# Attention and gated convolution on one core: batch 1's convolution on VectorE, in another written order of all engines

## The chip, the cores and the metric

The kernel runs on one core of a Trainium2 chip. The metric is the device time of one execution in microseconds (us), as the median of several runs. The core's engines are TensorE (PE in the profile, with its weight loads as PEld), VectorE (DVE), ScalarE (ACT), GpSimd (POOL) and SyncE (SP). Each works through its own queue in order; POOL and SP issue the transfers.

## The reference

There are 8 batches of 8 heads, 576 positions and 64 features a head; the feed-forward part has 1024 hidden features and a convolution of three taps. All inputs and the output are float32.

```python
def _attn_ref(q, k, v, g_norm):
    kv = np.einsum('bhsd,bhse->bhde', k, v)
    out = np.einsum('bhsd,bhde->bhse', q, kv)
    rms = np.sqrt(np.mean(out * out, axis=-1, keepdims=True) + 1e-06)
    return (out / rms * g_norm).astype(np.float32)

def _moe_ref(x, w_in, conv_w, w_out):          # x: (8, 576, 512), the heads side by side
    h = np.maximum(x @ w_in, 0.0)              # (8, 576, 1024)
    hp = ...                                   # h with one row of zeros ahead and behind
    for k in range(3):
        conv_out += conv_w[k][None, None, :] * hp[:, k:k + S, :]
    gate = 1.0 / (1.0 + np.exp(-conv_out))
    return (h * gate @ w_out).astype(np.float32)
```

## The kernel before

The whole program is one string of step names, `ORDER`, read from left to right. Each name calls a small function which issues its instructions, and at the end every engine is bound to the order in which it was given them. A name is a step with its indices; `@` gives the buffers or PSUM banks it takes, and `:` chooses an engine. So `kv.3.0.4@2` is the key-value product of batch 3, head pairs 0 to 3, into bank 2. A bank (there are eight) is free again when the step that empties it has run.

The steps, in the order in which one batch meets them (b is the batch, t a pair of heads, f a block of 128 hidden features, p a pair of batches):

- `Lq`, `Lk`, `Lv` load q, k and v of a batch (POOL issues them and they are cast to bfloat16 on the way, L301); `Li`, `Lo` load quarters of w_in and halves of w_out (L315, L322). Two buffers each for q, k and v are reused by later batches, so such a load waits for the last step that reads the buffer.
- `qt` (L380) transposes q on PE and `qc` copies the result out of PSUM; `qtp` (L388) is another form for batch 4. For batches 5 to 7 `dq` does it instead by a transposing transfer that SP issues (L436), behind the load of q.
- `kv` (L358) is k times v, 48 matmuls for a batch; `kvc`, `kvn`, `ky` copy it out, `kx` moves halves of it by a transfer.
- `ot` (L430, L431) or `oq` (L464) is q times that. `sq` (L493) squares it on ACT and `oc` copies it to SBUF.
- The norm: for batches 0 and 1 `on`, `nl`, `mu0`; later `ss` (sums of squares, L575), `ln` (root, L584), `sl` (its split into two bfloat16 parts, four DVE instructions, L591 to L594), `sp` (spreading on PE, L603), `mu` (L629). Batch 7's factors go through DRAM (`fw`, `fr`).
- `hm` (L640) is the hidden product, eight matmuls for a block of a batch; `re` is its relu (L646 on ACT, L648 on DVE).
- The convolution of a block pair on DVE: `ta` (two tap multiplies for a block, L699, L700), `aa` and `ab` (two additions, L706, L712); `sg` is the sigmoid on ACT (L745), `mg` the merge h times gate on DVE (L751). It is done by a group of batches: group 0 is batch 0, group 1 batch 1, group 2 batches 2 and 3, and so on. For blocks 6 and 7 of groups 0 and 1 `cm` (L731) does the convolution on PE with diagonal weights, six matmuls for a block, and `sg` reads PSUM (L742); `dg` makes those weights.
- `om` (L761) is the output product of 128 rows, in two halves of four matmuls for the first and last pair of batches and eight matmuls at once otherwise; `oh` (L776) is the very last one in two halves of its columns. `ea`, `eh` empty it into a row buffer, `st`, `sh` store it by SP.
- `unread` issues matmuls on constant data whose result nobody reads (fills, L427).

The lines by which a step's engine is chosen are these; in `copy` the engine is the caller's choice, which differs from step to step:

```python
    def copy(to, fr, on_act):
        if on_act:
            nc.scalar.activation(to, fr, AX.Copy)
        else:
            nc.vector.tensor_copy(to, fr)
    def relu(to, fr):
        if pick[0] == 0:
            nc.scalar.activation(to, fr, AX.Relu)
        else:
            nc.vector.tensor_scalar(to, fr, 0.0, None, op0=AL.max)
```

For `qc` and `qc0` the choice 1 is ACT; for `kvc`, `kvn`, `ky`, `oc`, `ea` and `eh` it is DVE. Whether a group's block uses the convolution on PE is decided by nothing but whether `cm` stands in the order for it.

Of the kernel before, what the change touches and what calls it, by code (L numbers as in the profile page):

```python
# [72 lines left out]
sqh.0.3.0@3 unread.3@3 onh.0.3.0@6 sqh.0.3.1 onh.0.3.1 nlh.0.3.0@3 muh.0.3.0 Lk.1.0@1 qt.1.0@0 nlh.0.3.1 qc.1.0:1@2
muh.0.3.1 Li.0 hm.0.2@6 re.0.2 ta.0.2@0 hm.0.3@4 re.0.3 hm.0.6@6 Lq.1.2 ta.0.3 Lv.1.2 re.0.6 aa.0.1 hm.0.7@4 Lk.1.2
Lq.2.0@0 cm.0.6@6 re.0.7:1 sg.0.6@1 kv.1.0.2@0 cm.0.7@4 kvc.1.0.2.0:1@1 kvc.1.0.2.1 sg.0.7 ot.1.0@0 hm.0.1@6 ab.0.1
sq.1.0@4 re.0.1 qt.1.1@4 hm.0.0@2 on.1.0@6 mg.0.3 qc.1.1@3 ot.1.1@4 nl.1.0@4 re.0.0:1 sq.1.1@5 kv.1.2.2@2
kvc.1.2.2.0 ta.0.0@1 mu0.1.0 kvc.1.2.2.1 on.1.1@6 Li.2 ot.1.2@2 nl.1.1@5 ot.1.3@0 ta.0.1 sq.1.2@6 mu0.1.1 aa.0.0
# [768 lines left out]
```

## Time and profile before

| what | value |
|---|---|
| median of 3 runs | 179.97 us (179.6 to 180.15) |
| span of the profiled execution | 177.6 us |
| that execution's own time | not recorded apart; the median is 2.4 us above the span |
| PE busy | 168.4 us, 95% of the span |
| ACT busy | 149.7 us, 84% |
| DVE busy | 139.5 us, 79% |
| POOL busy | 30.8 us, 17% |
| granted PE clock | 1.000 |

The span runs from the first to the last instruction of one execution under the profiler. Busy times are unions of instructions of an engine. A row of the chain of waits reads: start, length, what it was (an engine's line, or a transfer). A row of a timeline reads: start, length, engine, line, operation, output and input with their shapes, how many, and in brackets the idle time before it with what ended it. A row of the busy time by stretch reads: the stretch, its length, then the busy time of PE, PEld, DVE, ACT and POOL, the granted clock, the share of the transfer engines and GB/s. A row of the transfers ends with the median time from issue to landing. A row of the waits reads: who waited for whom, in total, how often, the longest.

### The profile page before, as it was taken

Reading aid. Unit: us, or ns where it says so; the run is one execution under the profiler, and the core shown is the slowest. Engines: PE = TensorE matmul, PEld = TensorE weight load, DVE = VectorE, ACT = ScalarE, POOL = GpSimd, SP = SyncE. Lnnn points to the kernel's source line nnn. Section 1 sums busy time; section 2 is a strip of 40 time slices with the busy share of each in tenths; the row PEclk is TensorE's granted clock in tenths of the full one; section 3 lists DMA queues with packets and bytes.
Section 4 is the critical chain, followed back from the end, with each engine's and each line's share of the span. In section 5 each row is a group of like instructions: output and inputs, shape, how many; then the busy total and the mean of one; then the engine's idle time right before and its main releaser. Section 6 shows DMA issues by size and latency. Waiting matters only on the chain.

```text
span 177.6 us, 4060 instructions
## 1 busy us (share of the span) xinstructions
PE 168.4 (95%) x1641; PEld 101.3 (57%) x1660; DVE 139.5 (79%) x235; ACT 149.7 (84%) x233; POOL 30.8 (17%) x54
## 2 busy tenths in 40 slices
PE   6989996999999999999999999999999999999992
PEld 2545753877545677753667764444677764444541
DVE  5665669999998898999799999939999999950000
ACT  2479899999999969999999999999989987764332
POOL 7995516402600013050000000000000000000000
PEclk9999999999999999999999999999999999999999
DMA  6999999999999999999999950197040003422696
GB/s 155 188 183 197 200 204 201 205 203 206 205 204 203 198 192 139 174 203 198 160 201 179 293 128 0 53 219 263 21 160 0 4 0 143 152 82 99 258 352 219
DMA packets 36219, 29.49 MB, mean 166 GB/s; under 512 B 8528, under 2 KB 31720, under 8 KB 36200
## 3 DMA queue, kind: packets, MB, share of 16 engines
q0 software_dynamic: 21760, 15.96, 59.5%
q1 hardware_dynamic: 14400, 13.26, 28.9%
q8 instruction: 13, 0.21, 0.4%
q14 instruction: 6, 0.05, 0.1%
q10 hardware_dynamic: 40, 0.01, 0.0%
HBM read 33.70 MB, written 9.58 MB: 244 GB/s over the span
## 4 chain that ended last, share of the span: by engine, by line
PE 70%; DMA 20%; POOL 4%; ACT 2%; issue 2%; POOLq 0%; ACTq 0%
PE bank L761 33%; PE bank L640 27%; DMA v_sb<-in_v_dram 10%; DMA k_sb<-in_k_dram 7%; DMA q_sb<-in_q_dram 4%; PE bank L358 3%; PE bank L464 2%; POOL q_sb L241 1%; PE bank L603 1%; PE bank L575 1%; POOL v_sb L241 1%; POOL k_sb L241 1%; PE bank L776 1%; PE bank L731 1%; PE bank L388 1%
## 5 line engine op out<-in xcount | busy, mean ns | idle before, releaser
L640 PE MATMUL bank<-xT,w_in_sb 128*128 128x288 bf16 x496 | 64.5, 286 | 0.1
L761 PE MATMUL bank<-w_out_sb,h 128*128 128x512 bf16 x268 | 63.0, 379 | 1.1 <-issue 0.6
L640 PEld LDWEIGHTS <-w_in_sb 128*128 128x128 bf16 x496 | 47.6, 98 | 14.1 <-issue 0.5
L761 PEld LDWEIGHTS <-h 128*128 128x128 bf16 x280 | 26.3, 98 | 30.6 <-issue 1.9
L646 ACT ACTIVATE h<-bank 128x576 bf16<-128x576 f32 x61 | 37.9, 657 | 4.2 <-PE bank L640 3.9
L745 ACT ACTIVATE taps<-taps,cwn 128x1152 bf16<-128x1152 bf16 (+1 forms) x36 | 38.2, 1094 | 0.1
L341 ACT ACTIVATE row<-bank 128x512 f32<-128x512 f32 (+1 forms) x37 | 21.3, 598 | 12.3 <-PE bank L761 9.3
L751 DVE TENSOR_TENSOR h<-h,taps 128x2304 bf16<-128x2304 bf16 (+1 forms) x20 | 22.2, 1113 | 2.0 <-ACT taps L745 1.2
L706 DVE TENSOR_TENSOR taps<-taps 128x2304 bf16<-128x2304 bf16 (+1 forms) x18 | 20.9, 1160 | 0.4
L712 DVE TENSOR_TENSOR taps<-taps,h 128x2304 bf16<-128x2304 bf16 (+1 forms) x18 | 20.8, 1153 | 0.3
L699 DVE TENSOR_SCALAR taps<-h,cwn 128x1152 bf16<-128x1152 bf16 (+1 forms) x36 | 16.7, 463 | 2.5 <-ACT h L646 2.4
L493 ACT ACTIVATE sq<-bank 128x576 bf16<-128x576 f32 x28 | 17.9, 676 | 0.0
L700 DVE TENSOR_SCALAR taps<-h,cwn 128x1152 bf16<-128x1152 bf16 (+1 forms) x36 | 17.5, 487 | 0.0
L629 DVE SCALAR_TENSOR_TENSOR xT<-o,cw,bank 128x576 bf16<-128x576 f32 x20 | 15.3, 809 | 2.7 <-PE bank L603 2.5
L341 ACT ACTIVATE o<-bank 128x576 f32<-128x576 f32 x22 | 15.0, 694 | 0.0
L213 ACT ACT_TABLE_LOAD x10 | 12.8, 1283 | 2.5 <-issue 2.4
L301 POOL DMA_DIRECT2D q_sb<-in_q_dram x8 | 6.2, 772 | 31.4 <-PE bank L388 16.6
L427 PE MATMUL bank<-fill 128*128 128x512 bf16 x25 | 9.0, 480 | 1.7 <-DVE fill L228 1.5
L358 PEld LDWEIGHTS <-k_sb 96*64 96x64 bf16 x384 | 7.3, 114 | 4.0 <-issue 2.6
L358 PE MATMUL bank<-v_sb,k_sb 96*64 96x64 bf16 x384 | 8.5, 199 | 1.0 <-DMA k_sb<-in_k_dram 0.7
L301 POOL DMA_DIRECT2D k_sb<-in_k_dram x8 | 6.1, 758 | 14.4 <-PE bank L358 12.5
L562 DVE SCALAR_TENSOR_TENSOR xT<-bank,cw,root 128x576 bf16<-128x576 f32 x7 | 5.6, 815 | 1.8 <-ACT root L542 1.7
(93 smaller groups left out, 135.3 us busy)
## 6 DMA issues: line engine op xcount, KB each, us to landing
out_dram<-row SPq DMA_DIRECT2D x35, 256.0 KB, 2.8
q_sb<-in_q_dram POOLq DMA_DIRECT2D x6, 576.0 KB, 13.7
k_sb<-in_k_dram POOLq DMA_DIRECT2D x6, 576.0 KB, 14.7
v_sb<-in_v_dram POOLq DMA_DIRECT2D x6, 576.0 KB, 16.3
factor<-factor SPq DMA_DIRECT2D x4, 288.0 KB, 4.9
w_in_sb<-in_moe_w_in_dram POOLq DMA_DIRECT2D x4, 256.0 KB, 8.7
w_out_sb<-in_moe_w_out_dram POOLq DMA_DIRECT2D x2, 512.0 KB, 18.0
q_sb<-in_q_dram POOLq DMA_DIRECT2D x4, 144.0 KB, 4.6
```

What stands on the lines that cost most here:

```text
L341: nc.scalar.activation(to, fr, AX.Copy)
L358: nc.tensor.matmul(ps[i][i * D:(i + 1) * D, t - t0, :], k_sb[:, 2 * t + i, r * D:(r + 1) * D], v_sb[:, 2 * t + i, r * D:(r + 1) * D], star ...
L493: nc.scalar.activation(in_order(b, s), product(b, t), AX.Square)
L640: nc.tensor.matmul(ps[:, e, :HS], w_in_sb[:, t, f * P:(f + 1) * P], x[:, t, e * HS:(e + 1) * HS], start=(t == 0), stop=(t == NT - 1))
L646: nc.scalar.activation(to, fr, AX.Relu)
L699: nc.vector.tensor_scalar_mul(tap[:, 0, f % 2, :n, 8:8 + S], h[:, f], cwn[:, 0, f:f + 1])
L700: nc.vector.tensor_scalar_mul(tap[:, 1, f % 2, :n, :S], h[:, f], cwn[:, 2, f:f + 1])
L706: nc.vector.tensor_add(tap[:, 1, :, :n, :S], tap[:, 0, :, :n, 7:7 + S], tap[:, 1, :, :n, 1:1 + S])
L712: nc.vector.tensor_add(y, y, h[:, 2 * j:2 * j + 2])
L745: nc.scalar.activation(y, y, AX.Sigmoid, scale=cwn[:, 1, f:f + 1])
L751: nc.vector.tensor_mul(h, h, T["tap", c, j][:, 1, :, :n, :S])
L761: nc.tensor.matmul(T["om", p, m], h[:, f, m * P:(m + 1) * P], w_out_sb[:, f, :], start=(f == 0), stop=(f == NF - 1))
```

## The change

Nothing but the string `ORDER` changes; every function stays. Batch 1's blocks 6 and 7 get `ta.1.6`, `ta.1.7`, `aa.1.3` and `ab.1.3` in place of `cm.1.6` and `cm.1.7`, so the whole convolution of batch 1 runs on VectorE. All steps stand in another order, banks and buffers are given out anew, and the loads of POOL and the transposing transfers of SP are in another sequence. The engine is another one for these steps: from ACT to DVE go 14 relus (`re.0.1`, `0.5`, `0.6`, `1.0`, `1.2`, `1.4`, `2.3`, `3.0`, `3.6`, `4.1`, `5.4`, `5.5`, `6.6`, `7.1`), `ea.0.5`, `1.1`, `1.6`, `2.1`, `3.0`, `3.4`, `3.5`, `eh.3.8.0`, `oc.2.3`, `4.3`, `7.1`, `7.3`, `qc0.0.1` to `0.3`, `kvc.1.0.2.1` and `kvn.5`; from DVE to ACT go `oc.2.0`, `oc.5.0`, `qc.2.1`, `qc.4.0`, seven `kvc`, `kvn.6`, `kvn.7` and both `ky.5`. There are 26 fills instead of 27.

POOL's loads after the first ten, before: Lq.1.0 Li.1 Li.3 Lv.1.0 Lk.1.0 Li.0 Lq.1.2 Lv.1.2 Lk.1.2 Lq.2.0 Li.2 Lk.2.0 Lv.2.0 Lq.3.0 Lk.3.0 Lv.3.0 Lo.0 Lo.1 Lq.4.0 Lq.5.0 Lk.4.0 Lv.4.0 Lk.5.0 Lv.5.0 Lq.7.0 Lv.7.0 Lk.7.0 Lk.6.0 Lv.6.0 Lq.6.0.

After: Lq.1.0 Li.3 Li.1 Lk.1.0 Lv.1.0 Lq.1.2 Li.0 Lv.1.2 Lk.1.2 Lq.2.0 Lk.2.0 Lv.2.0 Li.2 Lq.3.0 Lk.3.0 Lv.3.0 Lo.0 Lo.1 Lk.4.0 Lq.5.0 Lv.4.0 Lq.4.0 Lv.5.0 Lk.5.0 Lk.6.0 Lk.7.0 Lv.7.0 Lq.7.0 Lv.6.0 Lq.6.0.

The transposing transfers of SP, before: dq.5.0 dq.5.1 dq.7.0 dq.7.1 dq.6.0 dq.6.1; after: dq.5.1 dq.5.0 dq.7.0 dq.6.0 dq.6.1 dq.7.1.

The diff, cut to the start, the stretch from kv.1.2.2 to batch 1's last taps, the stretch around kv.6.0.4, and the end:

```diff
 ORDER = """
-pre@0,0,0 unread.10@0 qt0.0.0@0 ps pn pi ca.k.0 ca.v.0 kv.0.0.1@1 kvc.0.0.1.0:1@0 ct@2 qt0.0.1@3 qc0.0.0:1@0
...
-hm.0.5@0 sg.0.1 Lk.3.0@1 Lv.3.0@1 re.1.7 sg.0.0 pl ta.1.2@0 re.0.4 ta.1.3 re.0.5 hm.1.4@4 kv.2.0.4@2 Lo.0 aa.1.1
...
-oc.2.1 Lk.4.0@0 Lv.4.0@0 kv.3.0.4@2 re.1.0 ss.2@3 oc.2.3 mg.0.2 ln.8@0 aa.1.2 kvc.3.0.4.0:1@1 kvc.3.0.4.1:1 ab.1.2
...
-om.0.2.0@2 Lv.5.0@1 sg.1.5 sg.1.4 qtp.4.0@0 cm.1.6@6 qc.4.0@4 mg.1.2 ea.0.0@2 hm.2.5@4 sl.1@0 hm.2.2@0 sg.1.1
-om.0.2.4 re.2.5 sg.1.6@0 re.2.2 ea.0.2@3 sg.1.0 sp.3.0@6,4 cm.1.7@0 mu.3.0.1 mu.3.0.0 hm.2.4@2 hm.2.7@6 sg.1.7
...
+pre@0,0,0 ca.k.0 Lq.1.0@1 ca.v.0 pi unread.10@6 kv.0.0.1@0 unread.2@6 ct@1 qt0.0.1@2 al.h0@0 al.x0@0 Li.3 qt0.0.0@3
...
+ab.0.0 mu0.1.3 ps ha.1.2@4 qc.2.0@0 hb.1.2 sg.0.0 re.1.2:1 sg.0.1 hb.1.3 re.1.3 kv.2.0.4@0 mg.0.1 qt.2.1@2
+kvc.2.0.4.0@0 kvc.2.0.4.1 qc.2.1:1@1 ta.1.2@0 hm.0.4@4 ta.1.3 aa.1.1 mg.0.0 ot.2.0@0 ab.1.1 sq.2.0@0 hm.0.5@6 re.0.4
+hm.1.1@2 oc.2.0@0 re.0.5:1 ta.0.4@1 re.1.1:1 ot.2.2@4 sg.1.3 ot.2.1@0 sq.2.2@1 hm.1.4@6 oc.2.2@1 sq.2.1@2 hm.1.7@2
+hm.1.0@4 ta.0.5 re.1.4:1 aa.0.2 oc.2.1 sg.1.2 ot.2.3@0 re.1.7 ab.0.2 hm.1.5@6 qt.3.1@2 re.1.0:1 sq.2.3@3 Lk.3.0@1
+oc.2.3:1 Lv.3.0@1 Lo.0 Lo.1 kv.3.0.4@4 ss.2@5 mg.1.1 sg.0.4 sg.0.5 re.1.5 qt.3.0@0 hm.1.6@6 qc.3.1@0 mg.0.2
...
+re.2.4 hm.2.7@2 hm.2.5@6 re.2.7 mg.1.2 re.2.5 ab.1.0 sp.3.0@0,2 mu.3.0.1 sg.1.1 om.0.2.4 sg.1.0 mu.3.0.0 ta.1.6@0
...
+ab.2.3 hm.2.0@2 ea.0.6@5 re.2.0 aa.2.1 sl.2@0 ab.2.1 hm.3.1@0 sp.4.1@4,2 re.3.1 kv.7.0.4@6 mu.4.1.0 Lq.6.0@0 sg.2.3
+kvn.7.0.4 mu.4.1.1 sp.4.0@0,4 sg.2.2 mu.4.0.0 om.0.8.4 kx.7.0.4.0 hm.3.0@2 mu.4.0.1 al.h2@0 sp.5.0@0,4 kv.6.0.4@6
...
+sg.4.5 sg.4.4 aa.4.3 om.3.6.0@1 om.3.5.0@4 st.2.4 st.1.3 ab.4.3 sg.4.6 om.3.2.0@5 sg.4.7 ea.2.1:1@1 mg.4.2 om.2.6.0@7
+mg.4.3 om.3.1.4 om.3.2.4 om.3.3.4 om.3.6.4 om.3.5.4 st.2.8 st.2.7 ea.3.1@2 om.3.0.4 ea.3.2@4 st.2.3 ea.3.3@0
...
```

More of the change, by code (lines that the diff above doesn't have):

```diff
@@ L73 @@
[L73 to L77, printed above, removed]
@@ new lines @@
+sq.0.1@0 kvc.0.2.1.0 mu0.0.0 pl kvc.0.2.1.1 unread.1@2 on.0.1@0 ot.0.2@2 nl.0.1@1 mu0.0.1 qt0.0.3@4 unread.3@5
+kv.0.3.1@5,0 sq.0.2@0 qc0.0.3 kvc.0.3.1.1:1 Lq.1.2 kvc.0.3.1.0 on.0.2@6 nl.0.2@0 ot.0.3@4 sqh.0.3.0@0 unread.2@0
+onh.0.3.0@0 sqh.0.3.1 mu0.0.2 onh.0.3.1 Li.0 Lv.1.2 nlh.0.3.0@1 nlh.0.3.1 muh.0.3.0 muh.0.3.1 qt.1.0@6 qc.1.0:1@0
+hm.0.6@2 hm.0.2@0 re.0.2 al.h1@1 re.0.6:1 pn hm.0.7@4 hm.0.3@2 Lk.1.2 kv.1.0.2@0 ta.0.2@0 re.0.3 dg.6:1 dg.7:1
+cm.0.6@6 kvc.1.0.2.0@0 re.0.7:1 cm.0.7@2 kvc.1.0.2.1:1 sg.0.6@1 Lq.2.0@0 sg.0.7 qt.1.1@0 ta.0.3 qc.1.1@1 ot.1.0@4
@@ new lines @@
+ea.0.1@0 sp.2.1@2,6 mu.2.1.0 ot.3.3@0 mu.2.1.1 ea.0.3@1 om.0.0.0@5 sq.3.3@3 Lq.5.0@0 aa.1.2 oc.3.3 ss.3@4 sp.2.0@2,6
+mu.2.0.0 om.0.0.4 ln.1@0 ab.1.2 om.0.2.0@4 mu.2.0.1 sg.1.5 hm.2.4@0 Lv.4.0@0 ea.0.0@2 Lq.4.0@1 dq.5.1@2 sl.1@0 sg.1.4
+re.2.4 hm.2.7@2 hm.2.5@6 re.2.7 mg.1.2 re.2.5 ab.1.0 sp.3.0@0,2 mu.3.0.1 sg.1.1 om.0.2.4 sg.1.0 mu.3.0.0 ta.1.6@0
+hm.2.2@6 sp.3.1@2,0 kv.4.0.4@5 re.2.2 al.x2@1 ea.0.2@3 Lv.5.0@1 mu.3.1.1 kvn.4.0.4 qtp.4.1@6 ky.4.0.4.1 qtp.4.0@0
+ky.4.0.4.0 mu.3.1.0 hm.3.4@2 qc.4.0:1@0 hm.3.5@4 ta.1.7 re.3.4 qc.4.1@1 re.3.5 mg.1.0 oq.4.2@0 aa.1.3 ta.2.4@1
@@ new lines @@
+dq.5.0@3 sq.4.2@0 st.0.1 oq.4.0@2 ta.2.5 hm.2.6@6 oc.4.2@0 re.2.6 hm.3.6@4 sq.4.0@1 oc.4.0@1 ab.1.3 aa.2.2 hm.3.3@0
+sg.1.6 re.3.6:1 hm.3.7@6 Lk.5.0@1 re.3.3 om.0.5.0@2 ab.2.2 oq.4.3@0 sg.1.7 oq.4.1@4 mg.1.3 re.3.7 kv.5.0.4@3 sq.4.3@2
+oc.4.3:1 sq.4.1@3 oc.4.1 sg.2.4 kvn.5.0.4:1 ky.5.0.4.0 ky.5.0.4.1 hm.3.2@6 hm.2.3@0 om.0.5.4 ta.2.6@0 re.3.2 Lk.6.0@0
+Lk.7.0@1 om.0.7.0@4 oq.5.0@6 st.0.2 ta.2.7 sg.2.5 re.2.3:1 oq.5.2@0 om.0.7.4 ea.0.5:1@4 sq.5.2@4 aa.2.3 om.0.6.0@5
+oq.5.3@2 oc.5.2@2 sq.5.0@5 oq.5.1@0 Lv.7.0@0 oc.5.0@3 sq.5.3@6 mg.2.2 Lq.7.0@1 om.0.6.4 om.0.4.0@6 ss.4@7 sq.5.1@7
@@ new lines @@
+re.5.3 sq.7.1@1 hm.5.0@0 hm.5.5@6 hm.5.2@2 st.0.0 re.5.0 st.0.7 sg.2.6 aa.2.0 ab.2.0 oc.7.1:1 sg.2.1 sg.2.0 re.5.5:1
+hm.4.1@0 hm.4.5@4 re.4.1:1 kx.6.0.4.0 re.5.2 mg.2.3 hm.5.1@6 hm.5.4@0 re.4.5 st.0.8 mg.2.0 dq.6.1@1 kx.6.0.4.1
+oq.6.2@2 oq.6.0@4 re.5.4:1 re.5.1 sq.6.0@2 ta.3.2@0 hm.5.6@6 ta.3.3 om.1.1.0@0 dq.7.1@2 oc.6.0@1 oq.7.2@4 sq.6.2@3
+st.0.3 re.5.6 oc.6.2@2 aa.3.1 st.0.6 sq.7.2@4 oq.6.1@6 ea.1.1:1@0 oq.7.3@2 sq.6.1@5 ab.3.1 ta.3.0@1 om.1.3.0@1 oc.6.1
+oc.7.2@3 sq.7.3@6 ta.3.1 oq.6.3@6 om.1.6.0@0 oc.7.3:1 ea.1.6:1@1 om.1.5.0@4 sq.6.3@7 aa.3.0 hm.4.7@2 ss.6@0 sg.3.3
@@ new lines @@
+oc.6.3 ea.1.3@2 sg.3.2 mg.3.1 ss.7@1 ln.4@0 fw.4 ta.3.4@0 hm.5.7@6 re.5.7 ta.3.5 ln.3@0 ea.1.5@5 om.1.2.0@5 hm.4.6@6
+ab.3.0 ea.1.2@6 om.1.4.0@0 om.1.7.0@1 al.x3@0 st.1.1 aa.3.2 ea.1.4@0 re.4.7 sl.3@0 sp.6.0@2,4 re.4.6 ab.3.2 ea.1.7@7
+om.1.8.0@0 mu.6.0.0 sg.3.1 fr.7.1@0 sg.3.0 mu.6.0.1 sp.6.1@6,2 mu.6.1.0 mu.6.1.1 om.1.0.0@1 hm.6.0@4 sg.3.4 mu.7.1.0
+hm.6.5@2 fr.7.0@1 mg.3.0 hm.6.3@6 ta.3.6@1 mu.7.0.1 al.h3@1 mu.7.0.0 re.6.0 ta.3.7 st.0.4 hm.6.2@4 st.1.4 re.6.5
+re.6.3 hm.6.4@2 ea.1.8@0 st.1.2 re.6.2 re.6.4 st.0.5 mu.7.1.1 hm.6.1@6 st.1.5 aa.3.3 sg.3.5 st.1.6 hm.7.0@4 ab.3.3
@@ new lines @@
+ea.1.0@1 hm.7.5@2 hm.7.1@0 re.7.0 re.7.5 mg.3.2 re.7.1:1 sg.3.7 sg.3.6 hm.7.3@4 hm.7.2@2 re.6.1 re.7.2 mg.3.3 hm.7.6@0
+ta.4.0@0 re.7.3 ta.4.1 hm.7.4@6 st.1.8 hm.6.6@2 hm.7.7@4 re.7.6 re.7.4 om.2.2.0@0 om.2.5.0@1 om.2.3.0@6 aa.4.0
+re.6.6:1 ab.4.0 ta.4.2@1 sg.4.0 ta.4.3 aa.4.1 om.2.0.0@7 ea.2.3@0 om.2.4.0@6 sg.4.1 re.7.7 ea.2.5@3 ab.4.1 mg.4.0
+ta.4.4@0 hm.6.7@2 ta.4.5 om.2.8.0@1 ea.2.0@4 st.1.7 st.1.0 sg.4.2 sg.4.3 om.2.1.0@7 aa.4.2 ea.2.2@1 mg.4.1 st.2.0
+ta.4.6@1 om.2.7.0@0 ea.2.4@4 st.2.2 om.3.3.0@6 re.6.7 om.3.4.0@2 om.3.1.0@3 ea.2.8@5 ea.2.7@6 ta.4.7 om.3.0.0@0 ab.4.2
```

55 lines of the change are left out of this document (12 added, 43 removed).

## The prediction

> **What bounds the kernel now.** I read the page's head first, then the busy time by stretch, then the chain of waits, then the loads one by one, last the timelines of the engines for the price of single steps. Steps carry the names of the written order (kv.3.0.4 is batch 3's key-value product); a step "after" is one of the changed order.
>
> ```profile
> span 177.6 us, 4060 instructions
> PE 168.4 (95%) x1641; PEld 101.3 (57%) x1660; DVE 139.5 (79%) x235; ACT 149.7 (84%) x233; POOL 30.8 (17%) x54
> core 0: us, PE busy (x) PEld busy (x) DVE busy (x) ACT busy (x) POOL busy (x), PEclk, DMA share, GB/s
> 27.04:45.91 18.87, 17.26 (x264) 12.57 (x268) 18.39 (x35) 18.50 (x33) 7.18 (x17) 1.00 1.32 204
> 45.91:158.30 112.39, 111.32 (x1027) 67.17 (x1039) 103.13 (x145) 106.10 (x161) 6.38 (x8) 1.00 0.79 143
> 45.91:174.29 128.38, 127.17 (x1106) 74.98 (x1119) 103.72 (x145) 112.00 (x172) 6.38 (x8) 1.00 0.77 156
> 15.16 11.83 DMA k_sb<-in_k_dram
> 38.04 0.95 PE L358 MATMUL bank<-v_sb,k_sb 96*64 96x64 bf16 x48
> 28.67 17.11 DMA v_sb<-in_v_dram
> 45.91 0.95 PE bank L358 x48
> 96.88 0.88 PE bank L358 x48
> 173.38 0.89 PE bank L776 x8
> ```
>
> There are two regimes. Up to 45.91 the chain of waits runs through loads: the second half of batch 1's keys lands at 15.16 + 11.83 = 26.99, and batch 3's values, issued at 28.67, land at 45.78. The product that needs them, kv.3.0.4, is the piece at 45.91. It stands in PE's own order, so nothing written behind it can run earlier. From there to the end of the last output product, 173.38 + 0.89 = 174.3, PE is busy 127.17 of 128.38 us: it sets the pace. What follows, 177.6 − 174.3 = 3.3 us, is the last eviction and store. DVE is busy 103.13 of the 112.39 us up to 158.30, so it has 9.3 us to spare; ACT has 6.3. The granted clock is 1.00 in all rows.
>
> So the end is: when kv.3.0.4 starts, plus the PE work written behind it, plus what PE has to wait there, plus 3.3.
>
> **When kv.3.0.4 starts.** The 16 loads from batch 1 up to batch 3's values are the same ones in both orders, and Lv.3.0 is the last of them in both. The queue is never empty on the way (the stretch 27.04 to 45.91 moves 204 GB/s), so I let the values land at 45.8 again. Within the 16, Li.2 (the third quarter of w_in) goes behind Lv.2.0 instead of ahead of Lk.2.0.
>
> ```profile
> 17.07 0.78 POOL L301 DMA_DIRECT2D q_sb<-in_q_dram  x1 [1.24 <-PE bank L380]
> 17.84 0.77 POOL L315 DMA_DIRECT2D w_in_sb<-in_moe_w_in_dram  x1
> 21.03 0.77 POOL L301 DMA_DIRECT2D v_sb<-in_v_dram  x1 [0.52 <-DVE taps L706]
> q_sb<-in_q_dram POOLq DMA_DIRECT2D x1, 576.0 KB, 12.5
> w_in_sb<-in_moe_w_in_dram POOLq DMA_DIRECT2D x1, 256.0 KB, 12.9
> v_sb<-in_v_dram POOLq DMA_DIRECT2D x1, 576.0 KB, 15.6
> 30.79 1.33 PE L380 MATMUL bank<-ident,q_sb 96*64 96x96 bf16 x48 [0.29 <-ACT root L542]
> 127.36 13.83 PE bank L640 x112
> 57.05 0.74 PE bank L731 x6
> 10.58 0.81 PE L427 MATMUL bank<-fill 128*128 128x512 bf16 x3
> ```
>
> Issue and time to landing give: Lq.2.0 17.07 + 12.5 = 29.6, Li.2 17.84 + 12.9 = 30.7, Lv.2.0 21.03 + 15.6 = 36.6. Li.2 costs 1.1 us of the queue, so Lv.2.0 after lands at 35.5, and kv.2.0.4, which begins at 38.04 in the profile, can begin there. Li.2 then lands at 36.6; its first user, hm.0.4, is written behind kv.2.0.4 and 24 transposes, so not before 37.1, and loses nothing. Between it and kv.3.0.4 the order after has seven hidden products (56 matmuls of 13.83/112 = 0.1235: 6.9), the key-value product (0.9), 48 transposes (1.33) and four attention products of about 0.25: together 10.1, where before had four hidden products, 7.1, in 45.91 − 38.04 = 7.9. With the same 0.7 of loss, 35.5 + 10.1 + 0.7 = 46.3, a little behind the load: 46.2 is what I take, with 45.8 (the load itself) as the near end. The queries, keys and values of the stages before 27 are the same loads too, so I see no gain there. Costed at nothing are the moves of the setup steps (ps, pn, pl, ca) and of the evictions ahead of kv.2.0.4: they lie in the wait for those loads; uncovered, they cost at most their own durations, a few tenths each, and kv.2.0.4 has no spare time for more.
>
> **The PE work behind kv.3.0.4.** Batch 1's two convolutions on PE go (12 matmuls at 0.74/6: −1.5), three fills go ((0.81 − 0.38)/2 = 0.215 each, taking 0.38 as the last one's own duration: −0.6), one hidden product comes in because it was written ahead before (+1.0), and so do 24 transposes (+0.66). The sum is −0.5. The removed convolutions thus bring little: the PE work around the load was exchanged as well. 128.38 − 0.5 = 127.9.
>
> **What moves to DVE.** In place of the two PE convolutions stand four tap multiplies, two additions; and over the whole order 14 relus, seven output evictions and one half, two net o copies and three small query copies go from ACT to DVE, while two query copies and, net, nine small key-value copies go back to ACT. Each relu or eviction that DVE takes waits at the head of DVE's queue for PE's product; queued behind it are taps, additions and merges, for which ACT's sigmoids and then PE's output products wait. So DVE's idle time is what has to be weighed.
>
> ```profile
> 41.41 0.75 DVE L712 TENSOR_TENSOR taps<-taps,h 128x1152 bf16<-128x1152 bf16 x1
> 42.08 0.75 DVE L343 COPY o<-bank 128x576 f32<-128x576 f32 x1
> 42.74 1.41 DVE L343 COPY qT<-bank 128x1152 bf16<-128x1152 bf16 x2
> 44.07 0.36 DVE L699 TENSOR_SCALAR taps<-h,cwn 128x576 bf16<-128x576 bf16 x1
> 44.35 0.36 DVE L700 TENSOR_SCALAR taps<-h,cwn 128x576 bf16<-128x576 bf16 x1
> 44.63 0.75 DVE L648 TENSOR_SCALAR h<-bank 128x576 bf16<-128x576 f32 x1
> 45.30 0.75 DVE L751 TENSOR_TENSOR h<-h,taps 128x1152 bf16<-128x1152 bf16 x1
> 46.90 0.86 DVE L343 CAST kvbd<-bank 64x256 bf16<-64x256 f32 x2 [0.18 <-PE bank L358]
> DVE hi L591 <- ACT rs L584: 2.9, 1, 2.9
> DVE xT L629 <- PE bank L603: 2.5, 3, 1.0
> ```
>
> The steps follow one another closer than their durations: from start to start an addition takes 0.67, an o copy 0.66, a query copy 0.67, a tap multiply 0.28, a relu 0.67. An output eviction (512 wide, float32) has no row on DVE; between 0.5 and the o copy's 0.66 I take 0.66 × 512/576 = 0.59. Behind kv.3.0.4 and up to the last merge, mg.4.3, the order after has 8 relus more (5.4), 4 evictions (2.4), 2 o copies (1.3), a query copy (0.7), 8 tap multiplies (2.2; four of them only postponed), two additions and one merge (2.0), and five small copies of 0.43 fewer (−2.1): +11.9. DVE then has 103.1 + 11.9 = 115.0 us of work in that stretch. PE, up to the first product that needs mg.4.3 (om.3.1.4), has 127.9 less the eleven half-size products behind it (each like the row at 173.38, 0.89 with its end, so I take 9.6 for all): 118.3, losses included. So DVE may stand idle for 3.3 us there; in the profile it stood idle 9.3. The 2.9 for the first split of batch 6's norm is covered after (ab.3.0 and aa.3.2 are queued in front of it). That leaves 6.4 as one end; the other is 0, since DVE's spare time then needed no filling. I take 4.1, nearer the middle: the waits for PE's spreading products (2.5) stay, because one or two steps stand between split and product as before, and 1.6 for the rest. 4.1 − 3.3 = 0.8 us late at the end. ACT loses work and is no candidate.
>
> **The sum.** 46.2 + 127.9 + 0.8 + 3.3 = 178.2 us of span, 0.6 above the 177.6 of the profile. The page gives the profiled execution's span; the median of the three runs, 179.97, is 2.4 above it, which I carry as it is: 180.6.
>
> **Loads and transposing transfers.** The order of the loads after batch 3 changes too.
>
> ```profile
> 56.40 7.41 SPq L436 DMA_TRANSPOSE qT<-q_sb  x2
> 45.07 0.77 POOL L301 DMA_DIRECT2D v_sb<-in_v_dram  x1
> 65.74 0.77 POOL L301 DMA_DIRECT2D q_sb<-in_q_dram  x1 [16.55 <-PE bank L388]
> 77.90 0.77 POOL L301 DMA_DIRECT2D v_sb<-in_v_dram  x1
> v_sb<-in_v_dram POOLq DMA_DIRECT2D x1, 576.0 KB, 17.6
> q_sb<-in_q_dram POOLq DMA_DIRECT2D x1, 576.0 KB, 12.4
> v_sb<-in_v_dram POOLq DMA_DIRECT2D x1, 576.0 KB, 14.6
> ```
>
> With two transposing transfers issued from 56.40 on, three loads took from 62.7 (45.07 + 17.6) to 78.1 (65.74 + 12.4): 15.5 for what otherwise takes (45.8 − 36.6)/3 = 3.1 each at most, so 6.2 or about 3.1 for a transfer. Batch 6's values land at 77.90 + 14.6 = 92.5, the eleventh load behind Lo.1 in both orders, with three transfers ahead of it before. After, the third (dq.7.0) waits for Lq.7.0, the load just in front, so it lands between 89.4 and 92.5. PE needs them at kv.6.0.4: before 96.88 − 45.91 = 51.0 after kv.3.0.4, after 5.8 less (four hidden products, −4.0, and the two convolutions, fills, 24 transposes and eight small products of above), at 91.4. A wait of 0 to 1.1; I take none. By the Trainium skill (DMA: Bandwidth & Descriptors, Queues, rings and completion order) each DMA engine serves its queues in turn, packet by packet; sharing half and half, a transfer of 12 us would delay loads by 6, not by the 3.1 measured, and the wait would be up to 4.
>
> **The rivals.**
> 1. Faster: PE is at the load when it lands (−0.4), DVE never holds PE (−0.8), and PE's 1.2 us of visible idle behind 45.91 goes: 175.8, or 178.2 us. For it: ACT is as full in the profile (106.10 of 112.39) and PE lost little. Against: the fill-in of DVE was never that tight.
> 2. DVE becomes the bound: all 6.4 us of idle stay, 3.1 late instead of 0.8, and a second wait for spreading products as large as the first (2.5) keeps it from catching up: 180.5 to 183.0, so 183 to 185 us. It decides as soon as idle passes 3.3.
> 3. Late loads: kv.6.0.4 waits 1.1 on top of the forecast, and dq.7.0 behind it as much: 181.7 to 182.8.
> 4. A gap slows PE's clock. Between kv.1.2.2 (27.0) and kv.2.0.4 (35.5) the order after has only 4.4 us of PE work; in one piece the gap would be 4.1.
>
> ```profile
> 1.47 4.45 PE L427 MATMUL bank<-fill 128*128 128x512 bf16 x10 [1.47 <-DVE fill L228]
> ```
>
> The first ten fills took 4.45, twice 0.215 each. As long again at that rate after the gap would lose 2.2: 182.8. By the Trainium skill (TensorE: Matmul & The Clock Gate, Part 1) PE falls to half rate after an idle window of about 3.4 us. No gap of the profile is that long, and the steps of batch 1's norm split this one.
>
> **The chances.** Forecast 0.43 (its own range 179.8 to 181.5, a bit under half of it inside 0.3% of 179.97, which is 0.54 us and about what a measurement of this kernel tells from no change); rival 1 0.30; rival 2 0.13; rival 3 0.10; rival 4 0.04. Faster: nearly all of rival 1, 0.28. Same: the rest of it and 0.18 of the forecast, 0.20. Slower: 0.52. The range reaches from 178.4, within reach of rival 1, to 183.2, which leaves out the far part of rival 2.
>
> **What would show it.** Right: kv.3.0.4 at 46 or a little later, waiting for v_sb or just behind it; DVE above 150 us busy, ACT near 140; PE's wait ahead of om.3.1.4 between 0 and 2, released by DVE's merge; batch 6's values landed before kv.6.0.4. Wrong: kv.3.0.4 before 45 (then loads came sooner and my anchor falls), DVE idle over 8 behind 46, or a wait on a transposing transfer ahead of an oq step.

## The result, and the profile after

The changed kernel takes 180.48 us (median of 7 runs, 180.18 to 181.07), the kernel before 179.54 us on the same chip (7 runs, 179.13 to 180.15, the three of the table above among them). The ratio is 1.0053, with a 95% interval of 1.003 to 1.0077: slower by about 0.9 us. A second comparison, below, gives 1.0049. Here and below a ratio is estimated over all executions except the few in a slower state, so it differs a little from the quotient of the medians.

The string `ORDER` is one line shorter in the changed kernel, so each of its line numbers behind it is one lower (L357 is the L358 of the kernel before); runs that start from the kernel before keep its numbers. The head of the page of the changed kernel:

```profile
span 178.5 us, 4060 instructions
PE 166.3 (93%) x1629; PEld 100.3 (56%) x1647; DVE 154.4 (87%) x257; ACT 140.5 (79%) x217; POOL 30.7 (17%) x54
```

Its busy time by stretch (the columns are those of the kernel before):

```profile
27.33:46.09 18.76, 15.80 (x233) 10.97 (x236) 18.66 (x35) 17.72 (x30) 5.37 (x7) 1.00 1.32 205
46.09:164.14 118.05, 116.96 (x1080) 70.52 (x1087) 115.50 (x167) 102.76 (x153) 7.38 (x9) 1.00 0.76 149
46.09:173.97 127.88, 126.72 (x1131) 75.54 (x1138) 118.00 (x171) 106.12 (x159) 7.38 (x9) 1.00 0.74 153
```

DVE took over 14.9 us (139.5 to 154.4), ACT lost 9.2. Behind 46.09 PE is busy as before (126.72 of 127.88 us); DVE now fills 115.50 of the 118.05 us up to its last merge. The span is 0.9 us longer. PE is not the reason: its last product ends at 172.93 + 1.05 = 173.98, 0.3 us earlier than in the kernel before. Three products of keys and values on PE's timeline in the changed kernel (the second half of batch 1's, batch 2's and batch 3's), the load of batch 3's values on POOL's, its landing, and the chain of waits:

```profile
27.33 0.57 PE L357 MATMUL bank<-v_sb,k_sb 96*64 96x64 bf16 x24 [0.42 <-ACT root L541]
34.99 0.95 PE L357 MATMUL bank<-v_sb,k_sb 96*64 96x64 bf16 x48
46.09 0.92 PE L357 MATMUL bank<-v_sb,k_sb 96*64 96x64 bf16 x48
28.96 0.77 POOL L300 DMA_DIRECT2D v_sb<-in_v_dram  x1
```

```profile
v_sb<-in_v_dram POOLq DMA_DIRECT2D x1, 576.0 KB, 16.0
```

```profile
43.45 0.68 DVE taps L705
44.83 0.75 DVE h L647
46.83 0.75 DVE qT L342
...
172.93 1.05 PE bank L775 x8
174.00 0.38 ACT row L340
```

The chain between 24 and 58 us now runs through DVE, where before it ran through loads as far as 45.8: batch 3's values land at 28.96 + 16.0 = 44.98, 1.1 us before kv.3.0.4. From 58 us on it is nearly all PE, up to the last eviction.

What grew is the stretch behind PE's last product, from 3.3 to 178.5 − 174.0 = 4.5 us. SP's and DVE's timelines at the end, first of the changed kernel, then SP's of the kernel before:

```profile
171.43 3.66 SPq L794 DMA_DIRECT2D out_dram<-row  x4
175.19 0.40 SPq L789 DMA_DIRECT2D out_dram<-row  x1
171.86 0.69 DVE L342 COPY row<-bank 128x512 f32<-128x512 f32 x1 [0.84 <-DMA out_dram<-row]
173.07 0.69 DVE L342 COPY row<-bank 128x512 f32<-128x512 f32 x1 [0.52 <-DMA out_dram<-row]
```

```profile
172.46 1.91 SPq L795 DMA_DIRECT2D out_dram<-row  x3
174.70 0.33 SPq L790 DMA_DIRECT2D out_dram<-row  x1
```

The very last eviction (eh.3.8.1) ends at 174.00 + 0.38 = 174.38 in the changed kernel, but its store is issued only at 175.19. SP issues in the written order, and four stores of row blocks stand in front of it. Two of them are late because DVE stands idle for 0.84 and 0.52 us ahead of their evictions, ea.3.5 and ea.3.4: row buffers 0 and 3 are still being stored by st.3.3 and st.2.6 (the releaser is the transfer out of them). In the kernel before, SP had nothing left to issue when the last eviction was done, and issued at 174.70. So 0.8 us of the growth lie ahead of the last issue; the rest lies behind it, where the last store lands in 2.4 us instead of 1.9.

### The profile page after: what moved, and what is told of

Same layout as the page of the kernel before. It is cut to its first block, busy times and chain, and to the rows that moved or that the text cites. A ratio compares the mean times of both kernels' runs of the same rounds, so it can differ in the third digit from the quotient of the medians.

```text
span 178.5 us, 4060 instructions
## 1 busy us (share of the span) xinstructions
PE 166.3 (93%) x1629; PEld 100.3 (56%) x1647; DVE 154.4 (87%) x257; ACT 140.5 (79%) x217; POOL 30.7 (17%) x54
## 4 chain that ended last, share of the span: by engine, by line
PE 72%; DVE 20%; DMA 2%; issue 2%; ACT 1%; SPq 0%; ACTq 0%; DVEq 0%
PE bank L760 30%; PE bank L639 29%; PE bank L357 3%; DVE h L647 3%; DMA stg<-in_v_dram 2%; DVE taps L705 2%; DVE xT L561 2%; DVE qT L342 2%; DVE taps L699 2%; DVE taps L698 2%; PE bank L463 2%; DVE xT L628 2%; DVE taps L711 2%; DVE h L750 2%; PE bank L379 1%
## 5 line engine op out<-in xcount | busy, mean ns | idle before, releaser
L639 PE MATMUL bank<-xT,w_in_sb 128*128 128x288 bf16 x496 | 65.3, 286 | 0.9 <-DVE h L647 0.5
L744 ACT ACTIVATE taps<-taps,cwn 128x1152 bf16<-128x1152 bf16 (+1 forms) x38 | 39.8, 1082 | 4.9 <-DVE taps L711 4.8
L645 ACT ACTIVATE h<-bank 128x576 bf16<-128x576 f32 x47 | 29.8, 655 | 4.8 <-PE bank L639 4.5
L340 ACT ACTIVATE row<-bank 128x512 f32<-128x512 f32 (+1 forms) x29 | 16.5, 598 | 12.4 <-PE bank L760 7.6
L705 DVE TENSOR_TENSOR taps<-taps 128x2304 bf16<-128x2304 bf16 (+1 forms) x19 | 21.5, 1134 | 0.2
L711 DVE TENSOR_TENSOR taps<-taps,h 128x2304 bf16<-128x2304 bf16 (+1 forms) x19 | 21.5, 1130 | 0.2
L698 DVE TENSOR_SCALAR taps<-h,cwn 128x1152 bf16<-128x1152 bf16 (+1 forms) x38 | 18.1, 477 | 0.4 <-ACT h L645 0.3
L699 DVE TENSOR_SCALAR taps<-h,cwn 128x1152 bf16<-128x1152 bf16 (+1 forms) x38 | 18.3, 483 | 0.0
L647 DVE TENSOR_SCALAR h<-bank 128x576 bf16<-128x576 f32 x17 | 12.8, 751 | 0.9 <-PE bank L639 0.9
L340 ACT ACTIVATE o<-bank 128x576 f32<-128x576 f32 x20 | 13.2, 676 | 0.0
L342 DVE COPY row<-bank 128x512 f32<-128x512 f32 (+1 forms) x8 | 5.2, 653 | 7.1 <-PE bank L760 5.5
L357 PEld LDWEIGHTS <-k_sb 96*64 96x64 bf16 x384 | 7.3, 112 | 3.6 <-issue 3.2
L357 PE MATMUL bank<-v_sb,k_sb 96*64 96x64 bf16 x384 | 8.3, 197 | 0.7 <-ACT root L541 0.4
```

The source lines that it names most:

```text
L357: nc.tensor.matmul(ps[i][i * D:(i + 1) * D, t - t0, :], k_sb[:, 2 * t + i, r * D:(r + 1) * D], v_sb[:, 2 * t + i, r * D:(r + 1) * D], star ...
L639: nc.tensor.matmul(ps[:, e, :HS], w_in_sb[:, t, f * P:(f + 1) * P], x[:, t, e * HS:(e + 1) * HS], start=(t == 0), stop=(t == NT - 1))
L698: nc.vector.tensor_scalar_mul(tap[:, 0, f % 2, :n, 8:8 + S], h[:, f], cwn[:, 0, f:f + 1])
L699: nc.vector.tensor_scalar_mul(tap[:, 1, f % 2, :n, :S], h[:, f], cwn[:, 2, f:f + 1])
L705: nc.vector.tensor_add(tap[:, 1, :, :n, :S], tap[:, 0, :, :n, 7:7 + S], tap[:, 1, :, :n, 1:1 + S])
L711: nc.vector.tensor_add(y, y, h[:, 2 * j:2 * j + 2])
```

## The experiments

Ratios are to the kernel before, run in the same session on the same chip, with their 95% intervals. There were three sessions: the tail, the convolution alone in its first place, the convolution back on PE and the three early relus in the first; the changed kernel again, the later place, the five late relus and the first fills in the second; the rest in the third.

**The tail.** The late evictions get row buffers whose stores have long landed; nothing else changes. The diff is of the changed kernel:

```diff
-st.2.6 ea.3.5:1@0 ea.3.7@2 sh.3.8.0 ea.3.4:1@3
+st.2.6 ea.3.5:1@7 ea.3.7@4 sh.3.8.0 ea.3.4:1@2
```

> The changed order with other row buffers for three of its last evictions (ea.3.5 in row buffer 7 instead of 0, ea.3.4 in 2 instead of 3, ea.3.7 in 4 instead of 2), so that none waits for an earlier store to land; nothing else. Theory (the last stores): the profile of the changed kernel loses its time behind PE's end alone, because DVE waits 0.84 and 0.52 us for row buffers and the stores queue up on SP behind st.3.4; so the last store is issued at about 174.4 instead of 175.19, the span falls by 0.8 to 1.2 to about 177.4, and the time is 0.997 to 1.001 of before. Rival (the tail is set by the transfers themselves, four stores at the end share the transfer engines): the last landing moves by under 0.3 us and the ratio stays at 1.004 to 1.006. Rival (my prediction's step: DVE late at mg.4.3): nothing changes.

Measured: 178.95 us against 179.97, ratio 0.9951 (0.9931 to 0.997), a little faster than the 0.997 to 1.001 expected. The last rows of SP's and DVE's timelines in this run, and of its chain:

```profile
172.05 2.70 SPq L794 DMA_DIRECT2D out_dram<-row  x4
175.03 0.33 SPq L789 DMA_DIRECT2D out_dram<-row  x1
171.21 1.62 DVE L342 COPY row<-bank 128x256 f32<-128x256 f32 x3 [0.24 <-PE bank L775]
```

```profile
173.71 0.89 PE bank L775 x8
```

DVE's last three evictions now follow one another without a wait for a transfer, and the last store is issued 0.43 us behind PE's last product (173.71 + 0.89 = 174.60), as in the kernel before (0.43), against 1.21 in the changed one. The last store lands in 1.8 us again, and behind PE's last product the span has 177.8 − 174.6 = 3.2 us, as in the kernel before. The tail was the whole loss and more: without it the new order is faster than the kernel before. It was run once more later:

> The earlier tail alone, once more, as the yardstick of the two runs beside it: ratio 0.993 to 0.998, the last store issued 0.4 to 0.5 us behind PE's last product and landed 1.7 to 1.9 us after that.

Measured: 179.26 us against 179.78, ratio 0.9968 (0.9952 to 0.9984); last store again issued 0.43 us behind PE's last product. So this version beats both kernels, by 0.3 to 0.5%.

**The changed kernel again.**

> The changed kernel unchanged, as the yardstick of the runs beside it. Theory (the tail is its whole loss, 0.9 us of 178): ratio 1.003 to 1.007 against the kernel before, last store issued 1.1 to 1.3 us behind PE's last product. Rival (the first comparison was scatter of the loads): a ratio within 0.998 to 1.002, with batch 3's values landing earlier or later by as much.

Measured: 180.63 us against 179.79, ratio 1.0049 (1.0021 to 1.0078), with batch 3's values landed at 45.1 and the last store issued 1.27 us behind PE's last product (174.16 and 175.43). It was no scatter.

**The convolution alone, first place.** In the kernel before, batch 1's blocks 6 and 7 move to DVE, behind the split sl.1:

```diff
-cm.1.6@6 qc.4.0@4 mg.1.2 ... sl.1@0 hm.2.2@0 ... sp.3.0@6,4 cm.1.7@0 mu.3.0.1
+qc.4.0@4 mg.1.2 ... sl.1@0 ta.1.6@0 ta.1.7 aa.1.3 ab.1.3 hm.2.2@0 ... sp.3.0@6,4 sg.1.6 mu.3.0.1
```

> The order before with one part of the change alone: cm.1.6 and cm.1.7 taken out, and ta.1.6 ta.1.7 aa.1.3 ab.1.3 put behind sl.1, sg.1.6 and sg.1.7 a little later. PE loses 12 matmuls (1.5 us), DVE gains 2.45 us at about 60 us into the span. Theory (PE sets the pace behind kv.3.0.4 and DVE has spare time): faster by 0.8 to 1.4 us, ratio 0.992 to 0.996; not the full 1.5, since kv.4.0.4 can start only 1.2 us earlier before it meets its load (landed 62.7, started 63.9). Rival (DVE is the second bound there): mu.3 is pushed back by 1.7 us, hm.3 waits, and the ratio is 0.998 to 1.004.

Measured: 183.48 us, ratio 1.02 (1.0173 to 1.0227), far slower than either expectation. PE's timeline and the busy time by stretch of this run:

```profile
63.84 2.08 PE L640 MATMUL bank<-xT,w_in_sb 128*128 128x288 bf16 x8 [2.42 <-DVE xT L629]
```

```profile
64.00:70.00 6.00, 6.00 (x78) 4.19 (x77) 3.42 (x5) 2.14 (x5) 0.91 (x2) 0.50 1.30 180
```

The spreading factors (mu, L629) stand behind the new taps on DVE, and PE waits 2.42 us for the banks they free. Then the granted clock is 0.50 from 64 to 70 us: eight matmuls of a hidden product take 2.08 us. This run mixes two costs, the wait and the slow clock; the next place has only the first kind.

**The convolution alone, a later place.** The same steps behind qc.4.1, where DVE's queue comes to the taps of batches 2 and 3; the merge mg.1.3 and the two sigmoids go back with them:

```diff
-qc.4.1@2 ta.2.4@1 ta.2.5 ... oc.4.0@1 hm.3.6@2
+qc.4.1@2 ta.1.6@0 ta.1.7 aa.1.3 ab.1.3 ta.2.4@1 ta.2.5 ... oc.4.0@1 sg.1.6 sg.1.7 hm.3.6@2
```

> The kernel before with only batch 1's last two blocks convolved on VectorE: the two tap pairs and two additions stand behind qc.4.1, where DVE's queue is about to begin batches 2 and 3's taps, instead of ahead of the splits that PE waits for. Theory (PE sets the pace, and the earlier attempt at this lost by its place alone): 1.5 us of matmuls go, 0.5 to 1.3 us faster, ratio 0.993 to 0.998, and no PE wait over 1 us between 60 and 75 us. Rival (VectorE has no room for 2.6 us more behind 45.9 us, wherever it stands): ratio 1.000 to 1.010, with a PE wait released by DVE behind 62 us. If a wait over 2 us returns there, the granted clock falls again and the ratio goes to 1.02.

Measured: 181.78 us against 179.79, ratio 1.0112 (1.008 to 1.0144): slower, at the far end of the rival's range or just beyond it. The timelines of PE and DVE in this run, the last product in its chain, and the sum of its busy time over ten stretches from 62 to 104 us:

```profile
72.07 4.28 PE L640 MATMUL bank<-xT,w_in_sb 128*128 128x288 bf16 x32 [1.06 <-ACT h L646]
81.37 0.31 PE L464 MATMUL bank<-qT,kvx 64*64 64x288 bf16 x2 [0.48 <-DVE kvx L343]
66.41 0.41 DVE L699 TENSOR_SCALAR taps<-h,cwn 128x576 bf16<-128x576 bf16 x1
69.38 0.52 DVE L699 TENSOR_SCALAR taps<-h,cwn 128x1152 bf16<-128x1152 bf16 x1
```

```profile
176.55 0.89 PE bank L776 x8
```

```profile
sum 42.00, PE 39.18 PEld 25.30 DVE 39.59 ACT 38.06 POOL 4.60; mean PE 3.92 PEld 2.53 DVE 3.96 ACT 3.81 POOL 0.46
```

The same sum of the kernel before:

```profile
sum 42.00, PE 41.47 PEld 27.80 DVE 39.55 ACT 40.05 POOL 4.74; mean PE 4.15 PEld 2.78 DVE 3.96 ACT 4.00 POOL 0.47
```

The moved steps take 69.38 − 66.41 = 3.0 us on DVE. PE ends 3.2 us later (177.44 against 174.27) in this profile, whose execution took 182.50, 0.7 above the run's median; by the medians the loss is 2.0 us. In these 42 us DVE was busy 39.55 in the kernel before and 39.59 here: 2.4 us of idle time stayed, none of it was filled, and PE's idle time grew by 41.47 − 39.18 = 2.3 us. The 79% of the page is an average; in this stretch DVE took no more. The longest of PE's waits, 1.06 us, is released by a relu on ACT, and ACT was as full there before (40.05), so the two are not wholly separated by this run; the chain from 62 to 82 us runs through DVE for 88% of its length. The clock stayed at 1.00 after this run's wait of 1.06 us.

**The convolution back on PE, in the changed kernel.** cm.1.6 and cm.1.7 come back in place of ta.1.6, ta.1.7, aa.1.3 and ab.1.3; the order around them stays.

```diff
-mu.3.0.0 ta.1.6@0 ... ta.1.7 ... aa.1.3 ... ab.1.3 ... sg.1.6 re.3.6:1 ... sg.1.7
+mu.3.0.0 ... cm.1.6@2 sg.1.6@0 re.3.6:1 ... cm.1.7@4 ... sg.1.7
```

> The changed order with that one part undone: cm.1.6 and cm.1.7 on PE again (before sg.1.6 and sg.1.7), ta.1.6 ta.1.7 aa.1.3 ab.1.3 taken out; the rest as changed. Theory (PE is packed from 58 us on in the changed order, DVE only just keeps up): slower than the changed order by 1.3 to 1.7 us, ratio to before 1.012 to 1.016, PE's end at about 175.5. Rival (DVE is the bound of the changed order): the 2.45 us that DVE gets back outweigh, ratio 0.998 to 1.004.

Measured: 181.44 us, ratio 1.0102 (1.0064 to 1.014), a little under the 1.012 expected. The products of keys and values on PE's timeline, and the chain:

```profile
27.55 0.57 PE L357 MATMUL bank<-v_sb,k_sb 96*64 96x64 bf16 x24 [0.42 <-ACT root L541]
36.05 0.95 PE L357 MATMUL bank<-v_sb,k_sb 96*64 96x64 bf16 x48
46.15 0.92 PE L357 MATMUL bank<-v_sb,k_sb 96*64 96x64 bf16 x48
```

```profile
70.69 0.90 PE bank L730 x6
73.43 0.75 PE bank L730 x6
74.21 0.66 ACT taps L741
175.07 0.89 PE bank L775 x8
```

kv.3.0.4 starts at 46.2, as in the changed kernel, and PE ends at 175.96, 2.0 us later: the twelve matmuls (1.5 to 1.65) and 0.5 of a wait for the sigmoid that frees their bank. Its tail is short (last store issued at 176.39, 0.43 us behind PE), because with PE later one of the two waits for a row buffer is gone and the other is 0.38 us. So it is to be set against the earlier tail of the same session: 1.0102 against 0.9951, 2.7 us. In the new order the convolution on DVE thus saves 2 us or more, while in the old order it cost 2.0 us in the better of the two places tried: as far as these places show, the move pays only together with the rearrangement.

**Three early relus back on ACT** (re.0.5, re.1.2 and re.1.4 lose their `:1`), to see whether DVE sets the start of kv.3.0.4.

> The changed order with three of the moved relus (re.1.2, re.0.5, re.1.4) on ACT again, in the stretch in which the chain of waits of the changed kernel runs through DVE (24 to 58 us). Theory (DVE sets the start of kv.3.0.4 there, at 46.1, where its load landed at 45.0): kv.3.0.4 starts 0.5 to 1.1 earlier, and the end comes as much earlier, ratio 0.999 to 1.003. Rival (ACT is as full there, 4.5 to 5.0 us of every 5): ACT takes over as the bound, kv.3.0.4 starts at the same time or later, ratio 1.004 to 1.010.

Measured: 181.33 us, ratio 1.0099 (1.0063 to 1.0136). kv.3.0.4 starts at 46.8, no earlier, but in this profile batch 3's values landed at 46.5, so the load alone would have held it. DVE was relieved (7.27 of the 9.80 us up to 46.8), ACT was full:

```profile
37.00:46.80 9.80, 9.40 (x119) 6.88 (x113) 7.27 (x15) 9.76 (x19) 2.32 (x3) 1.00 1.29 204
```

The tail is the late one of the changed kernel, and the ratio is not clearly apart from that kernel's (1.003 to 1.0077). The rival's outcome came: with ACT full, giving DVE less does not help. The loads were late in this profile, too: kv.2.0.4 waited 0.79 us for batch 2's values.

What sets kv.3.0.4 in the changed order can be read from the nine other profiles of it. It starts 18.6 to 18.9 us behind kv.1.2.2 in all of them. In four of these the granted clock fell to about half between 32 and 36 us (the last section). There kv.2.0.4 starts later, 8.5 to 8.6 us behind kv.1.2.2 instead of 7.6 to 7.8, and kv.3.0.4 follows it after 10.1 to 10.3 us instead of 11.1; the run with the convolution back on PE is one of the four (36.05 − 27.55 = 8.50 and 46.15 − 36.05 = 10.10, against 7.66 and 11.10 in the changed kernel). So PE has slack of 0.8 us there and does not set the start. Nor does the load, which landed 0.5 to 1.8 us before it. DVE is busy 9.93 us of the 10 from 36 to 46 in all nine, ACT 9.5 to 9.9, and the chain of the changed kernel names DVE. That DVE paces this stretch, with ACT close behind, is thus argued by what is left; no run shortens DVE's work there without lengthening ACT's.

**Five late relus back on ACT**, with the earlier tail (re.4.1, 5.4, 5.5, 6.6 and 7.1 lose their `:1`):

> The changed kernel with the earlier tail of the first such run, and five late relus (4.1, 5.4, 5.5, 6.6, 7.1) back on ACT: DVE loses 3.4 us of work behind 95 us. Theory (DVE does not hold PE; mg.4.3 ends just in time): as the version with the earlier tail alone, ratio 0.993 to 0.998. Rival (the prediction's step: DVE is 0.8 us late at mg.4.3): 0.8 us faster than that, ratio 0.989 to 0.992. Third: ACT is now late with sigmoids or evictions: ratio 0.999 to 1.005 with a PE wait on ACT behind 100 us.

Measured: 182.3 us, ratio 1.013 (1.0102 to 1.0159): the third outcome, with more loss than expected. PE's timeline and the chain of this run:

```profile
104.18 2.12 PE L639 MATMUL bank<-xT,w_in_sb 128*128 128x288 bf16 x16 [1.06 <-ACT h L645]
107.58 1.14 PE L639 MATMUL bank<-xT,w_in_sb 128*128 128x288 bf16 x8 [0.91 <-ACT h L645]
141.93 3.10 PE L639 MATMUL bank<-xT,w_in_sb 128*128 128x288 bf16 x24 [0.62 <-ACT h L645]
```

```profile
100.17 2.04 ACT taps L744 x2
103.59 0.55 ACT h L645
```

The returned relus queue behind sigmoids (L744) on ACT, and PE waits 2.6 us for the banks. This does not tell whether DVE held PE, since ACT took its place.

**Two more evictions on DVE**, with the earlier tail, to measure how near DVE is to holding PE at om.3.1.4:

```diff
-om.3.1.0@3 ea.2.8@5 ea.2.7@6 ta.4.7
+om.3.1.0@3 ea.2.8:1@5 ea.2.7:1@6 ta.4.7
```

> The earlier tail, and two more evictions (2.8 and 2.7, 0.60 us each from start to start on DVE) ahead of the last taps on DVE. Theory (in the changed order mg.4.3 ends only about 0.25 us before PE comes to om.3.1.4): DVE is 1.2 later, PE waits 0.8 to 1.0 us for the merge ahead of om.3.1.4, ratio 0.998 to 1.003, 0.5% above the version with the earlier tail beside it. Rival (DVE has room to the end, and its 87% is only an average): no PE wait there and the same time as that version.

Measured: 180.82 us, ratio 1.0044 (1.0027 to 1.0062), against 0.9968 for the earlier tail alone beside it, so 1.4 us are lost, a little more than expected. PE's and DVE's timelines and the chain of this run:

```profile
165.55 4.92 PE L760 MATMUL bank<-w_out_sb,h 128*128 128x512 bf16 x22 [0.92 <-DVE h L750]
156.18 0.69 DVE L342 COPY row<-bank 128x512 f32<-128x512 f32 x1 [0.59 <-PE bank L760]
164.13 1.36 DVE L750 TENSOR_TENSOR h<-h,taps 128x2304 bf16<-128x2304 bf16 x1 [0.60 <-ACT taps L744]
```

```profile
173.94 0.89 PE bank L775 x8
```

The wait appeared where it was expected. From the start at 165.55 to PE's end at 174.83 are 9.28 us. In the changed kernel that puts om.3.1.4 at 173.98 − 9.28 = 164.70, while its last merge ended at 164.14: 0.56 us of margin. Two evictions and a wait of 0.59 for PE's product used that up. From kv.3.0.4 (45.71) to PE's end are 129.1 us here, against 127.7 with the earlier tail alone (46.85 to 174.59); the wait of 0.92 is the larger part of these 1.4 us, and the rest is not located.

**Fills against the clock**, with the earlier tail; the first try with the fills in bank 1, the second with each ahead of the product that writes the same bank (`unread.3@1 ot.1.2`, `unread.2@2 on.1.2`, `unread.2@6 on.1.3`). In the first the fills go over a part of what ot.1.3 left for heads 6 and 7 of batch 1, so its output is another one there; its work is the same.

> The changed kernel with the earlier tail, and six more fills (matmuls on constants that nobody reads) in the three gaps of PE between 28 and 32 us. Theory (small gaps there let the granted clock fall to half between 33 and 36 us in some executions, and that time is hidden in the wait for the loads): granted clock 1.00 in 32 to 36 us, time within 0.3% of the version with the earlier tail, ratio 0.993 to 0.998. Rival (the half clock costs): 0.5 to 1.0 us faster, ratio 0.989 to 0.992. If the clock still falls with the gaps filled, its cause lies elsewhere.

> The earlier tail, and six more fills between 28 and 32 us, each ahead of the product that writes the same bank, so that the output stays the reference's. Theory (the half clock behind 32 us is hidden in the wait for batch 2's values): granted clock 1.00 in 32 to 36 us and the time of the version with the earlier tail beside it within 0.3%. Rival (the half clock costs): 0.5 to 1.0 us faster than that version.

Measured: first 179.49 us, ratio 0.9975 (0.995 to 0.9999); second 179.28 us, 0.9969 (0.9952 to 0.9986), beside 0.9968 without fills. The clock was 1.00 between 32 and 36 us in both profiles; what it is without them is told in the last section. The medians agree, but without fills only about one execution in five has the half clock, so they could hardly show its cost. The profiles say more: with the half clock kv.2.0.4 came about 0.8 us later and kv.3.0.4 no later (above), so none of it reaches kv.3.0.4.

## Why the prediction was right, and where it was not

The forecast of 180.6 us stands beside 180.48, and the sign is right, but both by luck: the step that made the forecast slower did not happen, and the one that made the kernel slower was forecast as unchanged. Step by step:

- **kv.3.0.4 at 46.2**: 46.09, for another reason. The number was kv.2.0.4 at 35.5 and 10.8 us of PE's work and loss behind it; they were 34.99 and 11.10. The profiles with the half clock show that PE can do this work in 10.1 and is not what sets the start. The anchor beside it, the load at 45.8, was 0.8 too late (44.98). The prediction did not consider DVE here, which was busy 18.66 of 18.76 us and, as argued above, paces this stretch.
- **PE's work of 127.9 us behind it**: 127.88.
- **DVE 0.8 us late at mg.4.3**: wrong. The work was right: 115.0 us forecast, 115.50 busy up to 164.14. PE came to om.3.1.4 at 164.70, 118.6 behind kv.3.0.4 (forecast 118.3). The mis-sized term is DVE's remaining idle time: 4.1 taken, 118.05 − 115.50 = 2.55 measured, since the waits for spreading products, carried over as 2.5, nearly went (0.3 left). Instead of 0.8 us late the merge was 0.56 early. The prediction said that DVE decides as soon as its idle passes 3.3 us; the run with two more evictions shows such a point, near by.
- **3.3 us behind PE's last product, unchanged**: wrong, 4.5. Which row buffer an eviction takes, and which store still reads it, was not followed through the new order, although the seven evictions that change engine were counted. The earlier tail shows this term by itself.
- **2.4 us from span to median**: about 2.0 (180.48 − 178.5; the profiled execution itself took 180.26). In the executions of all experiments the time is 1.7 to 1.9 us above the execution's own span, so about 0.6 of the 2.4 was scatter between the profiled execution of the kernel before and the median of three.

So 0.8 too much for DVE and 0.4 in the offset stood against 1.2 too little for the tail; the total is nearer than its terms. Without the 0.8 the same sum would have forecast the kernel 0.2 us faster. Of the rivals, the faster one had one of its three reasons right (DVE does not hold PE); PE's 1.2 us of small idle stayed (127.88 − 126.72), and the tail, which it did not have, took more than it gained. DVE as the bound did not come, with 0.56 us to spare. Late loads did not come: kv.6.0.4 started at 91.11 (forecast 91.4), released by PE's own work.

```profile
76.67 0.77 POOL L300 DMA_DIRECT2D v_sb<-in_v_dram  x1
91.11 0.95 PE L357 MATMUL bank<-v_sb,k_sb 96*64 96x64 bf16 x48
```

Batch 6's values landed at 90.3, inside the 89.4 to 92.5 that the price of 3.1 us for a transposing transfer gave; since it was issued 1.2 us earlier than before (76.67 against 77.90), this is no sharp test of that price. What half-and-half sharing would have made of it, 6 us for a transfer and up to 4 of wait, did not show. By the Trainium skill (DMA: Bandwidth & Descriptors, Queues, rings and completion order) a DMA engine goes from queue to queue by whole packets; equal shares follow from that only for packets of equal length, and the landing at 90.3 without a wait does not show them. The clock rival did not decide the time.

## What to carry to other kernels

When evictions change engine or order near the end, follow each row buffer to the store that still reads it, and the store queue to the last store: here three buffer numbers were worth over 1 us, more than the change itself. An engine's share of the whole span says nothing about its room in a stretch: at 79% DVE could not take 3 us in either of two places, at 87% in another order it could. Before an engine is given more, look in that stretch at whether its idle time can be filled or consists of waits that will stay.

## What the runs showed of the hardware beyond this

The granted clock can halve after less idle time than the prediction supposed. It did so after the 2.42 us of wait in the first convolution run. It also did so in the profile of the changed kernel run again, behind PE waits of no more than 0.77 us each between 27 and 32 us. The stretches and PE's timeline of that run, and then the stretch of the earlier tail run again:

```profile
32.00:34.00 2.00, 2.00 (x30) 1.44 (x26) 2.00 (x4) 1.97 (x3) 0.00 (x0) 0.52 1.34 202
34.00:36.00 2.00, 2.00 (x12) 1.27 (x10) 1.97 (x5) 2.00 (x4) 0.00 (x0) 0.63 1.38 200
```

```profile
27.68 0.57 PE L357 MATMUL bank<-v_sb,k_sb 96*64 96x64 bf16 x24 [0.43 <-ACT root L541]
30.11 0.19 PE L429 MATMUL bank<-sq,ones 128*128 128x64 bf16 x1 [0.77 <-ACT sq L492]
30.99 0.20 PE L429 MATMUL bank<-sq,ones 128*128 128x64 bf16 x1 [0.47 <-DVE xT L561]
```

```profile
32.00:34.00 2.00, 1.70 (x32) 1.35 (x32) 2.00 (x4) 1.98 (x3) 0.05 (x1) 1.00 1.34 201
```

In the first profile of the changed kernel the same waits (0.42, 0.77 and 0.48) were followed by a clock of 1.00, so these waits alone do not decide it. Over all executions with the earlier tail alone, 5 of 23 had a mean clock of 0.99 or less; with the six fills none of 22 (0.997 at the least). That is a weak difference at these counts, but it agrees with the profiles: neither of the two with fills has the half clock. What it takes lies in time in which PE otherwise waits there: kv.2.0.4 comes about 0.8 us later, and kv.3.0.4 does not. By the Trainium skill (TensorE: Matmul & The Clock Gate, Part 1) the clock falls after an idle window of about 3.4 us that runs freely, not from the kernel's start; that the same waits end in one state or the other fits a free-running window, that 2.42 us was enough does not fit the length, and here the measurement decides.

The landing of the same load in the same order of loads scatters by more than the change moved: batch 3's values landed at 45.0 us in the changed kernel and at 46.1 in the first run of the earlier tail (45.1 in the second), two kernels that differ only behind 164 us. Most of it, 0.8 us, already lies between the issues (28.96 and 29.75).
